# A spectral filter with a gated convolution on one core: low parts of y subtracted by GpSimd in the last 13 blocks, and the last two blocks' convolution taken one block at a time

## The chip, the core and the metric

The kernel runs on one core of a Trainium2 chip. The core has five engines that run side by side, each through its own list of instructions in a fixed order: TensorE (PE, matrix products), VectorE (DVE), ScalarE (ACT), GpSimd (POOL) and SyncE (SP, which here only starts transfers). They wait for each other through semaphores. SBUF is the on-chip memory of 128 partitions; TensorE writes its products to PSUM, a second on-chip memory, from which VectorE and ScalarE fetch them. The metric is device time in microseconds (us) from the first to the last instruction of one execution.

## The reference

```python
def _attn_ref(x, w_r, w_i, b_r, b_i):
    X = np.fft.rfft(x, axis=1)
    Yr = Xr @ w_r - Xi @ w_i + b_r
    Yi = Xr @ w_i + Xi @ w_r + b_i
    Yr = np.sign(Yr) * np.maximum(np.abs(Yr) - lam, 0.0)   # Yi alike, lam = 0.01
    y = np.fft.irfft(Y, n=x.shape[1], axis=1)

def _moe_ref(x, w_val, conv_w, w_out):          # x is the y above
    for k in range(K):                           # K = 5
        gate_pre += conv_w[k][None, None, :] * xp[:, k:k + S, :]
    gate = 1.0 / (1.0 + np.exp(-gate_pre))
    val = x @ w_val
    return (gate * val @ w_out).astype(np.float32)
```

x has 8 batches of 3200 positions and 256 channels, in float32. Each batch is transformed along its positions, mixed with complex 256 x 256 matrices, shrunk towards zero, and transformed back to y. Then a causal convolution of five taps per channel, through a sigmoid, gates the product of y with w_val; the gated values are multiplied by w_out.

## The kernel before

The Fourier transform is done by matrix products in two stages (64 x 50 positions), through two scratch tensors in DRAM (a_dram and z_dram). The result of the way back stands in SBUF as y_sb, channels on partitions. What follows is done in 8 blocks a batch, each of 400 positions in 2 halves of 128 channels, so 800 elements a partition. A block is written (b, k): batch b, block k, both from 0. The last two batches are 6 and 7.

For each pair of blocks, `conv` makes the gate's argument in a tile `acc`: ScalarE multiplies by the first tap (L1017), VectorE adds four taps for each channel half (L1020: one instruction of 800 elements, y_sb and acc in SBUF), and ScalarE takes the sigmoid (L1030). For each block, `gated` makes the values v_ps = y @ w_val on TensorE, VectorE multiplies them with the sigmoid (L1054, "the gate": v_ps in PSUM, acc in SBUF), and TensorE makes the output product o_ps with w_out, which ScalarE copies (L1079) and SyncE stores. The very last block's copy is shared by ScalarE and VectorE (L1073).

The products of matrices have two forms. In the split form a value is held as a high part, a rounded copy in a shorter format made by ScalarE (`split`, L505), and a low part, the difference, subtracted by VectorE (L507); twelve products of 400 columns (high x high, low weight x high, high weight x low, for two channel halves each way; L1003) make a block. In the whole-word form TensorE takes y or the gated product as it stands, with whole-word weights `w_late` that GpSimd sums once from their parts (L1090); four products, which appear as eight in the trace (L999), make a block and no split is needed. `LATE` lists the 16 blocks of the last two batches. The values of `LATE[6:]`, ten blocks, and the output products of `LATE[14:]`, two blocks, are in the whole-word form.

The order on each engine is found by the class `Plan` while the program is built: every piece of work has a due time `at`, an engine and a cost in ns, and a list schedule gives each engine's order. Due times come from the table `O`. The costs are the planner's own; what the chip takes stands in the trace. The split tile y_hl has two buffers, so the split of a block can run ahead of the product by two.

The first 752 us hold the forward and backward transforms of all batches, interleaved with the blocks of the batch before. After that only blocks (6, 3) and later are open.

Of the kernel before, what the change touches and what calls it, by code (L numbers as in the profile page):

```python
# [104 lines left out]
class Plan:  # L105
# [11 lines left out]
    def add(self, at, engine, busy, fn, uses=(), sets=(), new=None, delay=None, mode="r", kb=0, chain=None, extra=0, dmas=1, read=True, pair=None):  # L117
        n = len(self.pieces)
        before = set()
        for key in uses:  # L120
            before |= set(self.writers.get(key, ()))
        for key in sets:
            before |= set(self.readers.get(key, ())) | set(self.writers.get(key, ()))
        for key in uses:
            self.readers.setdefault(key, []).append(n)
        for key in sets:
            self.writers[key], self.readers[key] = [n], []
        p = dict(n=n, at=at, engine=engine, busy=busy, fn=fn, before=before, new=new or {}, mode=mode, kb=kb, extra=extra, dmas=dmas, read=read, pair=pair,
                 tiles={key[:2] for key in (*uses, *sets)}, delay=busy + LAND[engine] if delay is None else delay)
        p["behind"] = {self.last[chain]} if chain in self.last else set()  # L130
        if chain:
            self.last[chain] = n
        self.pieces.append(p)
        return n
# [159 lines left out]
def dve(n, copy=False):  # L294
    return 67 + n / (1.92 if copy else 0.96)


def act(n, kind="copy"):
# [23 lines left out]
     'val': 3.9688,  # L322
     'gate': -49.7775,
     'project': 6.045,
     'late_val': 6.023,
     'late_out': 14.484,
     'turn': -90.4451,
     'pre': -5.7976,
     'mix_sum': -1.2289,
# [11 lines left out]
     'u_val': 7,  # L341
     'u_conv': 8,
     'u_out': 9,
     'const': 1.7737,
     'load_x_0': 6.2588,
     'load_x_2': 11.2939,
     'load_x_3': 1.4455,
# [96 lines left out]
def fourier_filter_then_gated_conv(ctx: ExitStack, tc: tile.TileContext, x, w_r, w_i, b_r, b_i,  # L444
# [3 lines left out]
    sb = ctx.enter_context(tc.tile_pool(name="sb", bufs=2))  # L448
    ps = ctx.enter_context(tc.tile_pool(name="ps", bufs=1, space=bass.MemoryType.PSUM))
    dram = ctx.enter_context(tc.tile_pool(name="dram", bufs=2, space=bass.MemoryType.DRAM))  # L450
    LATE_VAL, LATE_OUT = set(LATE[int(O["late_val"]):]), set(LATE[int(O["late_out"]):])
    plan = Plan(SLOTS)
    add = plan.add
# [2 lines left out]
    def f32(ap):  # L456
        return ap.bitcast(F32)
# [37 lines left out]
    def two_banks(key, tag="ps_2"):  # L495
        return buffer(key, tag, [P, 2, 512])

    def split(at, n, key, src, high, low, uses=(), new=None, first=None):

        hl = key + ("high",), key + ("low",)  # L500

        def cast():
            if first:
                first()
            nc.scalar.copy(out=high(), in_=src())  # L505
        add(at, "ACT", act(n, "cast"), cast, uses, [hl[0]], new, chain=key[0])
        add(at + 0.001, "DVE", dve(n), lambda: nc.vector.tensor_tensor(out=low(), in0=src(), in1=f32(high()), op=ALU.subtract),  # L507
            [*uses, hl[0]], [hl[1]])
        return hl

# [173 lines left out]
    def of(name, b):  # L684
        return O[name] + O.get(f"{name}_{b}", 0.0)
# [254 lines left out]
    def y_at(k, c, tap=H0):  # L940
        return y_of(k, tap)[:, c]
# [64 lines left out]
    def conv(b, kk, at):  # L1006
        k = 2 * kk
        here = sorted({*y_keys(k, 1), *y_keys(k + 1, 1)})
        kg = ("acc", (b, kk))
        w = 2 * MB * N2  # L1010
        acc = lambda c: tl[kg][:, c]
        wide = lambda c, j: pair(y_sb, (MB * k + j) * N2, (N1 - 2 * MB - 2 * MB * k) * N2, w)[:, c]

        def first(c):
            if c == 0:
                tl[kg] = room(kg, "acc", 4 * TB).rearrange("p (c h n) -> p c h n", c=2, h=NH)
            nc.scalar.mul(acc(c), wide(c, 0), cw_sb[:, c, 0:1])  # L1017

        def tap(c, j):
            nc.vector.scalar_tensor_tensor(out=acc(c), in0=wide(c, j), scalar=cw_sb[:, c, j:j + 1], in1=acc(c), op0=ALU.mult, op1=ALU.add)  # L1020
        for c in range(2):
            add(at + of("conv", b) + 0.01 * c, "ACT", act(2 * TB, "conv"), lambda c=c: first(c), [*here, ("cw", 0, 0)],
                [kg + (c, e) for e in range(2)], {kg: "acc"} if c == 0 else None, chain="conv")
        for j in range(1, KC):
            for c in range(2):
                add(at + of("conv", b) + 0.02 * j, "DVE", 61 + dve(2 * TB), lambda c=c, j=j: tap(c, j), here,
                    [kg + (c, e) for e in range(2)],
                    delay=961 + (130 if j == KC - 1 else 0))
        for c in range(2):
            add(at + of("conv", b) + 0.15, "ACT", act(2 * TB, "sigmoid"), lambda c=c: nc.scalar.activation(  # L1030
                out=acc(c), in_=acc(c), func=AF.Sigmoid), (), [kg + (c, e) for e in range(2)])

    def gated(b, k, at):
        bk = (b, k)
        here = y_keys(k, 0)
        ky, kg, kv, kh, kp, ko = (("y_hl", bk), ("acc", (b, k // 2)), ("v_ps", bk), ("gated", bk), ("o_ps", bk), ("o", bk))
        if bk in LATE_VAL:
            vs = [*here, ("w_late", 0, 0)]
            vm = lambda e: matrix(kv, e, lambda: w_late[0], lambda h, c: y_at(k, c), True)
        else:  # L1040
            src = lambda: y_of(k)
            view = lambda j: tl[ky][:, j].rearrange("p c (h n) -> p c h n", h=NH)
            vs = [*split(at + of("y", b), 2 * TB, ky, src, lambda: view(0), lambda: view(1), here, {ky: "y_hl"},
                         lambda: buffer(ky, "y_hl", [P, 2, 2, TB], F32R)), ("w", "w_val", "high"), ("w", "w_val", "low")]
            vm = lambda e: matrix(kv, e, wv_sb, lambda h, c: tl[ky][:, h, c, :], False)
        for e in range(2):
            add(at + of("val", b), "PE", 1344 if bk in LATE_VAL else 1101, lambda e=e: vm(e), vs, [kv + (e,)],
                {kv: "ps_2"} if e == 0 else None, chain="val")


        ours = [kg + (c, k % 2) for c in range(2)]
        part = lambda: pair(tl[kg].rearrange("p c h n -> p c (h n)"), k % 2 * MB * N2, (3 - 2 * (k % 2)) * MB * N2, MB * N2)
        by_half = lambda ap: ap.rearrange("p c (h n) -> p c h n", h=NH)
        add(at + of("gate", b), "DVE", dve(2 * TB), lambda: nc.vector.tensor_tensor(  # L1054
            out=part(), in0=by_half(tl[kv][:, :, 0:TB]), in1=part(), op=ALU.mult), [kv + (0,), kv + (1,)], ours)
        if bk in LATE_OUT:
            gs = [*ours, ("w_late", 0, 0)]
            om = lambda e: matrix(kp, e, lambda: w_late[1], lambda h, c: part()[:, c], True)
        else:
            gs = [*split(at + of("gate", b) + 0.1, 2 * TB, kh, part, lambda: by_half(tl[kh][:, 0]), lambda: by_half(tl[kh][:, 1]),  # L1060
                         ours, {kh: "g_hl"}, lambda: buffer(kh, "g_hl", [P, 2, 2, TB], F32R)),
                  ("w", "w_out", "high"), ("w", "w_out", "low")]
            om = lambda e: matrix(kp, e, wo_sb, lambda h, c: tl[kh][:, h, c, :], False)
        for e in range(2):
            add(at + of("project", b), "PE", 1344 if bk in LATE_OUT else 1101, lambda e=e: om(e), gs, [kp + (e,)],
                {kp: "ps_2"} if e == 0 else None)
        cols = out[b].rearrange("(c p) n -> p c n", p=P)
        dst = [cols[:, :, lo:lo + MB * N2] for lo in (k * TB, (NB - 1 - k) * TB + MB * N2)]
        kind = at + of("project", b) + 0.1
        if bk == (B - 1, NB - 1):  # L1070
            def keep(e):
                o = buffer(ko, "o", [P, 2, TB]) if e == 0 else tl[ko]
                (nc.scalar.copy, nc.vector.tensor_copy)[e](out=o[:, e], in_=tl[kp][:, e, 0:TB])  # L1073
            for e, eng in enumerate(("ACT", "DVE")):
                add(kind, eng, act(TB) if e == 0 else dve(TB), lambda e=e: keep(e), [kp + (e,)], [ko + (e,)],
                    {ko: "o"} if e == 0 else None)
                add(kind, "SP", 700, lambda e=e: [nc.sync.dma_start(out=dst[h][:, e], in_=block(tl[ko][:, e])[:, h]) for h in range(NH)], [ko + (e,)], (), kb=200, dmas=2, read=False)
            return
        add(kind, "ACT", act(2 * TB), lambda: nc.scalar.copy(out=buffer(ko, "o", [P, 2, TB]), in_=tl[kp][:, :, 0:TB]),  # L1079
            [kp + (0,), kp + (1,)], [ko + (0,)], {ko: "o"})  # L1080
        add(kind, "SP", 900, lambda: [nc.sync.dma_start(out=dst[h], in_=blocks(tl[ko])[:, :, h]) for h in range(NH)], [ko + (0,)], (), kb=400, dmas=2, read=False)
# [117 lines left out]
```

## Time and profile before

| | |
|---|---|
| time, median of 3 runs | 847.21 us (846.08 to 847.69) |
| the profiled execution's own time | 845.59 us |
| its span on the core | 843.8 us |
| TensorE busy | 825.3 us (98%) |
| VectorE busy | 735.9 us (87%) |
| ScalarE busy | 596.3 us (71%) |
| GpSimd busy | 147.9 us (18%) |
| granted TensorE clock | 0.993 of full speed |

Times in the trace's views are in us from the span's start, and a row gives start, duration, engine, line, operation, and output <- inputs. A group's row gives a count (x48), the busy time, the mean of one in ns, and the idle time just before with what ended it. TensorE's rows overlap, since its products are pipelined; the chain of waits shows what each added. GpSimd's busy time before is nearly all the issue of transfers; after 642 us it has nothing more to do.

### The profile page before, as it was taken

Reading aid. Unit: us, or ns where it says so; the run is one execution under the profiler, and the core shown is the slowest. Engines: PE = TensorE matmul, PEld = TensorE weight load, DVE = VectorE, ACT = ScalarE, POOL = GpSimd, SP = SyncE. Lnnn points to the kernel's source line nnn. Section 1 sums busy time; section 2 is a strip of 40 time slices with the busy share of each in tenths; the row PEclk is TensorE's granted clock in tenths of the full one; section 3 lists DMA queues with packets and bytes.
Section 4 is the critical chain, followed back from the end, with each engine's and each line's share of the span. In section 5 each row is a group of like instructions: output and inputs, shape, how many; then the busy total and the mean of one; then the engine's idle time right before and its main releaser. Section 6 shows DMA issues by size and latency. Waiting matters only on the chain.

```text
span 843.8 us, 24474 instructions
## 1 busy us (share of the span) xinstructions
PE 825.3 (98%) x10036; PEld 715.3 (85%) x10036; DVE 735.9 (87%) x1006; ACT 596.3 (71%) x903; POOL 147.9 (18%) x284
## 2 busy tenths in 40 slices
PE   9999989999999999999999999999999999999997
PEld 5777768888889889898989988898888899999775
DVE  3367796989988999989988999889989899979994
ACT  2246566787877787778787777778775778777662
POOL 5332222201221121302211031301212000000000
PEclk9899999999999999999999999999999999999999
DMA  8898999867877786767966696758875455336313
GB/s 191 246 238 229 266 230 271 224 173 223 241 187 199 204 225 193 196 171 219 266 204 173 180 251 194 222 144 217 249 211 157 136 154 161 108 100 172 109 64 98
DMA packets 122665, 162.33 MB, mean 192 GB/s; under 512 B 16496, under 2 KB 102266, under 8 KB 122554
## 3 DMA queue, kind: packets, MB, share of 16 engines
q1 hardware_dynamic: 109706, 134.73, 57.1%
q0 software_dynamic: 12848, 26.04, 12.0%
q8 instruction: 80, 1.31, 0.7%
q14 instruction: 31, 0.25, 0.1%
HBM read 82.06 MB, written 78.64 MB: 190 GB/s over the span
## 4 chain that ended last, share of the span: by engine, by line
PE 75%; DVE 14%; DMA 6%; ACT 2%; issue 2%; POOL 1%; SPq 0%; DVEq 0%; ACTq 0%; POOLq 0%
PE y_ps L903 14%; PE o_ps L1003 13%; PE v_ps L1003 11%; PE y_p L969 9%; PE y_ps L907 7%; DVE acc L1020 4%; PE z_ps L858 4%; PE s L789 4%; PE p L716 4%; PE v_ps L999 3%; DMA x<-in_x 3%; DMA a_dram<-s 2%; DVE s L736 2%; PE p L480 1%; DVE xs L838 1%
## 5 line engine op out<-in xcount | busy, mean ns | idle before, releaser
L1020 DVE SCALAR_TENSOR_TENSOR acc<-y_sb,cw_sb,acc 128x800 f32<-128x800 f32 x256 | 262.4, 1044 | 31.7 <-ACT acc L1017 30.1
L903 PE MATMUL y_ps<-w_sb,xs 128*128 128x256 f32 x1152 | 153.0, 284 | 2.0 <-DVE y_ps L909 1.7
L903 PEld LDWEIGHTS y_ps<-w_sb,xs 128*128 128x128 f32 x1152 | 142.5, 189 | 12.3 <-issue 5.6
L1003 PE MATMUL o_ps<-gated,wo_sb 128*128 128x400 f32 x744 | 150.7, 350 | 0.2 <-DVE s L736 0.2
L1003 PEld LDWEIGHTS o_ps<-gated,wo_sb 128*128 128x128 f32 x744 | 133.5, 188 | 5.7 <-issue 2.3
L1003 PE MATMUL v_ps<-y_hl,wv_sb 128*128 128x400 f32 x648 | 130.0, 347 | 0.4 <-ACT y_sb L973 0.4
L671 POOL DMA_DIRECT2D x<-in_x x142 | 74.5, 530 | 295.2 <-PE p L723 286.1
L1003 PEld LDWEIGHTS v_ps<-y_hl,wv_sb 128*128 128x128 f32 x648 | 114.8, 188 | 4.0 <-ACT sx L830 0.8
L736 DVE TENSOR_TENSOR s<-p,s 128x512 f32<-128x512 f32 (+2 forms) x144 | 88.6, 624 | 28.9 <-ACT s L731 16.9
L671 POOL DMA_DIRECT2D a_dram<-s x122 | 63.9, 528 | 196.9 <-DVE s L736 166.6
L969 PE MATMUL y_p<-g_sb,zl 100*64 100x100 f32 x2048 | 96.5, 251 | 0.8 <-ACT acc L1030 0.8
L915 ACT ACTIVATE tp<-y_ps,nlam 128x512 f32<-128x512 f32 (+1 forms) x104 | 69.8, 671 | 38.5 <-PE y_ps L903 37.0
L969 PEld LDWEIGHTS y_p<-g_sb,zl 100*64 100x64 f32 x2048 | 88.9, 137 | 9.5 <-issue 4.7
L907 PEld LDWEIGHTS y_ps<-w_sb,xs 128*128 128x128 f32 x576 | 76.4, 189 | 21.3 <-issue 8.9
L907 PE MATMUL y_ps<-w_sb,xs 128*128 128x256 f32 x576 | 87.7, 289 | 5.2 <-ACT y_ps L885 2.8
L917 DVE SCALAR_TENSOR_TENSOR tp<-y_ps,tp 128x512 f32<-128x512 f32 (+1 forms) x104 | 68.4, 661 | 7.1 <-ACT tp L915 6.9
L505 ACT CAST gated<-acc 128x800 fp32r<-128x800 f32 x62 | 53.5, 863 | 27.4 <-DVE acc L1054 27.0
L729 ACT COPY s<-p 128x512 f32<-128x512 f32 x64 | 37.5, 595 | 42.4 <-PE p L723 31.6
L716 PE MATMUL p<-x,f_sb 50*64 50x512 f32 x256 | 65.5, 599 | 1.3 <-DMA x<-in_x 0.8
L723 PE MATMUL p<-x,f_sb 50*64 50x512 f32 x240 | 65.9, 601 | 0.0
L1054 DVE TENSOR_TENSOR acc<-v_ps,acc 128x800 f32<-128x800 f32 x64 | 62.8, 981 | 3.4 <-PE v_ps L999 1.7
L1079 ACT COPY o<-o_ps 128x800 f32<-128x800 f32 x63 | 51.9, 823 | 19.2 <-PE o_ps L1003 13.9
(95 smaller groups left out, 1172.0 us busy)
## 6 DMA issues: line engine op xcount, KB each, us to landing
out<-o SPq DMA_DIRECT2D x126, 200.0 KB
a<-a_dram SPq DMA_DIRECT2D x96, 256.0 KB
z_dram<-z_t SPq DMA_DIRECT2D x48, 512.0 KB
zl<-z_dram SPq DMA_DIRECT2D x64, 384.0 KB
x<-in_x SPq DMA_DIRECT2D x63, 192.0 KB
a_dram<-s POOLq DMA_DIRECT2D x61, 192.0 KB, 4.3
a_dram<-s SPq DMA_DIRECT2D x59, 192.0 KB
x<-in_x POOLq DMA_DIRECT2D x57, 192.0 KB, 5.2
```

Source lines behind the costliest of these rows:

```text
L671: eng.dma_start(out=out[lo:hi], in_=in_[lo:hi])
L716: nc.tensor.matmul(p[k * HP:(k + 1) * HP, 0, :], f1_sb[half(0), 0:HP], xt[half(0), k * 512:(k + 1) * 512], start=True, stop=True)
L723: nc.tensor.matmul(dst, f1_sb[half(1), 0:HP], back[:, 2 * k:2 * k + 2, :], start=True, stop=True)
L736: nc.vector.tensor_tensor(out=st()[lo:hi, h, n], in0=p[lo:hi, 0, n], in1=st()[lo:hi, 1, n], op=(ALU.add, ALU.subtract)[h])
L903: nc.tensor.matmul(p[:, 1 - r, :], xm(hx, c, r, i), w_sb[:, m, hw, c, :], start=False, stop=k == 5, skip_group_check=True)
L907: nc.tensor.matmul(tl[ky][:, 0], sm(hx, c, i), w_sb[:, 0, hw, c, :], start=False, stop=k == 5, skip_group_check=True)
L915: nc.scalar.activation(out=buffer(kt, "tp", [P, 2, D])[:, 0:n], in_=tl[ky][:, 0:n], func=AF.Relu, bias=nlam)
L917: add(at + 0.2, "DVE", dve(n * D), lambda: nc.vector.scalar_tensor_tensor(out=tl[kt][:, 0:n], in0=tl[ky][:, 0:n], scalar=LAM, in1=tl[kt][: ...
L969: nc.tensor.matmul(dst[e * HP:(e + 1) * HP], zt[0:Q, m, c * P + e * HP:c * P + (e + 1) * HP], g, start=True, stop=True)
L1003: nc.tensor.matmul(p[:, e, 0:TB], w[:, hw, c, e * P:(e + 1) * P], src(hy, c), start=n == 0, stop=n == 5)
L1020: nc.vector.scalar_tensor_tensor(out=acc(c), in0=wide(c, j), scalar=cw_sb[:, c, j:j + 1], in1=acc(c), op0=ALU.mult, op1=ALU.add)
L1054: add(at + of("gate", b), "DVE", dve(2 * TB), lambda: nc.vector.tensor_tensor(out=part(), in0=by_half(tl[kv][:, :, 0:TB]), in1=part(), op= ...
```

## The change

Four things are edited.

1. `late_pool` is 3: for the blocks of `LATE[3:]`, that is (6, 3) to (6, 7) and the whole of batch 7, thirteen in all, the low part of y is subtracted by GpSimd instead of VectorE. The planner costs that at 4.9 ns an element.
2. `late_val` is 16: no block's values are in the whole-word form any more. The ten blocks that were get a cast on ScalarE and a subtract on GpSimd.
3. `late_out` is 12: the output products of the last four blocks, not two, are in the whole-word form.
4. The last pair's convolution is made by `conv_last`, block by block: each tap is an instruction of 400 elements for one block instead of 800 for the pair, and the second block is due 2.0 later.

```diff
-     'late_val': 6.023,
-     'late_out': 14.484,
+     'late_val': 16,
+     'late_out': 12,
...
+     'conv_last': 2.0, 'late_pool': 3, 'const': 1.7737,
...
+    LATE_POOL = set(LATE[int(O["late_pool"]):])
...
-    def split(at, n, key, src, high, low, uses=(), new=None, first=None):
+    def split(at, n, key, src, high, low, uses=(), new=None, first=None, pool=False):
...
-        add(at + 0.001, "DVE", dve(n), lambda: nc.vector.tensor_tensor(out=low(), in0=src(), in1=f32(high()), op=ALU.subtract),
+        eng, busy = ("POOL", 4.9 * n) if pool else ("DVE", dve(n))
+        add(at + 0.001, eng, busy, lambda: (nc.gpsimd if pool else nc.vector).tensor_tensor(out=low(), in0=src(), in1=f32(high()), op=ALU.subtract),
             [*uses, hl[0]], [hl[1]])
...
+        if (b, k) == (B - 1, NB - 2):
+            for i in range(2):
+                conv_last(b, k + i, at, kg)
+            return
...
+    def conv_last(b, k, at, kg):
+        here = y_keys(k, 1)
+        at += O["conv_last"] * (k % 2)
...
+        for c in range(2):
+            add(at + of("conv", b) + 0.01 * c, "ACT", act(TB, "conv"), lambda c=c: nc.scalar.mul(acc(c), y_at(k, c, 0), cw_sb[:, c, 0:1]),
+                [*here, ("cw", 0, 0)], [kg + (c, k % 2)], {kg: "acc"} if c == 0 and k % 2 == 0 else None, chain="conv")
+            for j in range(1, KC):
+                add(at + of("conv", b) + 0.02 * j, "DVE", 61 + dve(TB), lambda c=c, j=j: nc.vector.scalar_tensor_tensor(
+                    out=acc(c), in0=y_at(k, c, j), scalar=cw_sb[:, c, j:j + 1], in1=acc(c), op0=ALU.mult, op1=ALU.add),
+                    here, [kg + (c, k % 2)], delay=61 + dve(TB) + (190 if j == KC - 1 else 60))
...
-                         lambda: buffer(ky, "y_hl", [P, 2, 2, TB], F32R)), ("w", "w_val", "high"), ("w", "w_val", "low")]
+                         lambda: buffer(ky, "y_hl", [P, 2, 2, TB], F32R), bk in LATE_POOL), ("w", "w_val", "high"), ("w", "w_val", "low")]
```

On every engine the order is the one of before up to the split of block (6, 3), at about 753 us; from there to the end it is laid anew. In the changed kernel the lines have moved: the taps are L1022 (L1051 in `conv_last`), the gate L1078, the subtracts L509, the split products L1005, the whole-word products L1001.

VectorE's list around blocks (6, 3) to (6, 5), before: `acc` with taps is the convolution, `acc<-v_ps` the gate, `gated` the subtract of the gated product and `y_hl` that of y.

```order
L1054 TENSOR_TENSOR acc<-v_ps,acc 128x2x400
L507 TENSOR_TENSOR y_hl<-y_sb,y_hl 128x800
L507 TENSOR_TENSOR gated<-acc,gated 128x800
L1020 SCALAR_TENSOR_TENSOR acc<-y_sb,cw_sb,acc 128x800
L1054 TENSOR_TENSOR acc<-v_ps,acc 128x2x2x200
L507 TENSOR_TENSOR y_hl<-y_sb,y_hl 128x800
L1020 SCALAR_TENSOR_TENSOR acc<-y_sb,cw_sb,acc 128x800
L507 TENSOR_TENSOR gated<-acc,gated 128x800
```

The same place of the change:

```order
L1078 TENSOR_TENSOR acc<-v_ps,acc 128x2x400
L509 TENSOR_TENSOR gated<-acc,gated 128x800
L1022 SCALAR_TENSOR_TENSOR acc<-y_sb,cw_sb,acc 128x800
L1078 TENSOR_TENSOR acc<-v_ps,acc 128x2x2x200
L1022 SCALAR_TENSOR_TENSOR acc<-y_sb,cw_sb,acc 128x800 x2
L509 TENSOR_TENSOR gated<-acc,gated 128x800
```

The subtracts of y are gone from VectorE's list. They stand on GpSimd's, behind the sum of the late weights; the waits at a row's end name the engines waited for.

```order
L1114 TENSOR_TENSOR w_late_8760<-wv_sb_72 128x512 [waits DMAHW1_49,DMAHW0_49,PE_49]
L1114 TENSOR_TENSOR w_late_8760<-wo_sb_73 128x512
L509 TENSOR_TENSOR y_hl_10165<-y_sb_78,y_hl_10165 128x800 [waits DVE_49,Activation_49]
L509 TENSOR_TENSOR y_hl_10233<-y_sb_78,y_hl_10233 128x800 [waits DVE_49,Activation_49]
L509 TENSOR_TENSOR y_hl_10283<-y_sb_78,y_hl_10283 128x800 [waits Activation_49]
```

There are 13 such rows to the program's end, each waiting for ScalarE's cast, and nothing else on GpSimd among them.

TensorE's list at the end, before (v_ps are the values, o_ps the output products):

```order
L1003 MATMUL o_ps<-gated,wo_sb 128x400 x12
L999 MATMUL v_ps<-y_sb,w_late 128x400 x6
L1003 MATMUL o_ps<-gated,wo_sb 128x400 x12
L999 MATMUL v_ps<-y_sb,w_late 128x400 x2
L999 MATMUL o_ps<-acc,w_late 128x400 x8
```

and of the change:

```order
L1005 MATMUL o_ps<-gated,wo_sb 128x400 x12
L1005 MATMUL v_ps<-y_hl,wv_sb 128x400 x12
L1001 MATMUL o_ps<-acc,w_late 128x400 x4
L1005 MATMUL v_ps<-y_hl,wv_sb 128x400 x12
L1001 MATMUL o_ps<-acc,w_late 128x400 x4
```

The values come from split parts up to the last block, and the output products of blocks (7, 4) and (7, 5) have become whole-word ones; those of the last two blocks follow them as before.

More of the change, by code (lines that the diff above doesn't have):

```diff
@@ L343 @@
      'u_out': 9,
-     'const': 1.7737,
+     'conv_last': 2.0, 'late_pool': 3, 'const': 1.7737,
      'load_x_0': 6.2588,
@@ L1031, in conv, with acc @@
                 out=acc(c), in_=acc(c), func=AF.Sigmoid), (), [kg + (c, e) for e in range(2)])
+    def conv_last(b, k, at, kg):
+        here = y_keys(k, 1)
+        at += O["conv_last"] * (k % 2)
+        def acc(c):
+            if kg not in tl:
+                tl[kg] = room(kg, "acc", 4 * TB).rearrange("p (c h n) -> p c h n", c=2, h=NH)
+            return pair(tl[kg].rearrange("p c h n -> p c (h n)"), k % 2 * MB * N2, (3 - 2 * (k % 2)) * MB * N2, MB * N2)[:, c]
+        for c in range(2):
[5 more added lines that the diff above has]
+                    here, [kg + (c, k % 2)], delay=61 + dve(TB) + (190 if j == KC - 1 else 60))
+            add(at + of("conv", b) + 0.15, "ACT", act(TB, "sigmoid"), lambda c=c: nc.scalar.activation(out=acc(c), in_=acc(c), func=AF.Sigmoid),
+                (), [kg + (c, k % 2)])
     def gated(b, k, at):
```

## The prediction

> **What bounds the kernel now.** I read the page first: its busy line, its slices, and the shares of the chain that ended last.
>
> ```profile
> span 843.8 us, 24474 instructions
> PE 825.3 (98%) x10036; PEld 715.3 (85%) x10036; DVE 735.9 (87%) x1006; ACT 596.3 (71%) x903; POOL 147.9 (18%) x284
> DVE  3367796989988999989988999889989899979994
> POOL 5332222201221121302211031301212000000000
> PE 75%; DVE 14%; DMA 6%; ACT 2%; issue 2%; POOL 1%; SPq 0%; DVEq 0%; ACTq 0%; POOLq 0%
> ```
>
> TensorE is the bound as a whole, and GpSimd is idle in the last nine slices. But all that the change edits lies after 752 us, so its price must be read there. The view of busy time by stretches gives, in columns, the length, then PE, PEld, DVE, ACT and POOL, each with its instructions:
>
> ```profile
> 760.00:780.00 20.00, 20.00 (x206) 19.23 (x205) 20.00 (x24) 13.88 (x19) 0.00 (x0) 1.00 0.59 168
> 780.00:800.00 20.00, 20.00 (x135) 15.51 (x134) 19.93 (x22) 14.26 (x18) 0.00 (x0) 1.00 0.34 103
> 800.00:820.00 20.00, 20.00 (x135) 15.51 (x134) 19.18 (x21) 11.93 (x16) 0.00 (x0) 1.00 0.26 83
> 752.80:834.75 81.95, 81.95 (x592) 67.86 (x592) 75.50 (x81) 52.02 (x68) 0.00 (x0) 1.00 0.38 116
> ```
>
> The reader is to see two full engines. The last line is the stretch that I use: from the end of the last spectral work to the end of the last gate product. TensorE has no gap in its 81.95 us, VectorE hardly more than 6.5. Taking time off TensorE alone gains only what VectorE can follow; time put on VectorE costs soon. The chain in order of time (start, us, what) shows TensorE's steps:
>
> ```profile
> 773.57 2.18 PE v_ps L1003 x12
> ...
> 816.42 2.69 PE v_ps L999 x8
> 819.11 2.17 PE o_ps L1003 x12
> ...
> 833.71 5.39 PE o_ps L999 x16
> 839.10 0.03 ACTq L1073
> ```
>
> A block's values cost 2.18 us from split parts and 2.69 from whole words, and an output product from split parts 2.17.
>
> **TensorE's part of the change.** Ten blocks leave the whole-word form: 10 x (2.69 - 2.18) = 5.1 us less. Two more output products enter it: 2 x (2.69 - 2.17) = 1.0 more. Net 4.1 us less, and worth that only while TensorE stays the bound.
>
> **VectorE's own work.** Its groups in that stretch, and some of its rows in order of time:
>
> ```profile
> L1020 DVE SCALAR_TENSOR_TENSOR acc<-y_sb,cw_sb,acc 128x800 f32<-128x800 f32 x48 | 48.5, 1043 | 3.0 <-ACT acc L1017 2.9
> L1054 DVE TENSOR_TENSOR acc<-v_ps,acc 128x800 f32<-128x800 f32 x15 | 14.8, 984 | 3.4 <-PE v_ps L999 1.7 <-ACT acc L1030 0.9 <-PE v_ps L1003 0.7
> L507 DVE TENSOR_TENSOR gated<-acc,gated 128x800 fp32r<-128x800 f32 x14 | 13.8, 982 | 0.0
> L507 DVE TENSOR_TENSOR y_hl<-y_sb,y_hl 128x800 fp32r<-128x800 f32 x3 | 2.9, 982 | 0.0
> ```
>
> ```profile
> 768.65 5.86 DVE L1020 SCALAR_TENSOR_TENSOR acc<-y_sb,cw_sb,acc 128x800 f32<-128x800 f32 x6
> 774.43 0.98 DVE L1054 TENSOR_TENSOR acc<-v_ps,acc 128x800 f32<-128x800 f32 x1
> 775.33 1.04 DVE L1020 SCALAR_TENSOR_TENSOR acc<-y_sb,cw_sb,acc 128x800 f32<-128x800 f32 x1
> ...
> 833.75 0.99 DVE L1054 TENSOR_TENSOR acc<-v_ps,acc 128x800 f32<-128x800 f32 x1 [1.21 <-PE v_ps L999]
> ```
>
> Successive rows overlap a little, so I cost by distance of starts: a tap (774.43 - 768.65) / 6 = 0.96, a gate or subtract 775.33 - 774.43 = 0.90. By these the stretch holds 48 x 0.96 for taps, 15 x 0.90 for gates, 13 subtracts of the gated product (the first of the 14 lies before it) and 3 of y (16 x 0.90), and 0.3 for a copy: 74.3 us, which leaves 7.6 free. The change removes the 3 subtracts of y and 2 of the gated product: 5 x 0.90 = 4.5. The last two blocks' taps become 16 of half length for 8 whole ones; a 400-element tap has no row, and I take half of 0.96 with at most 0.06 more each, 0 to 1 us in all. VectorE's own work falls to 70 us. ScalarE gains ten casts of y and loses two of the gated product, all under 0.9 us: 52.02 becomes some 60 of 82, still hidden.
>
> **GpSimd's part, the one that decides.** Thirteen subtracts of 800 elements, both inputs in SBUF, are new on GpSimd. The page has one pair of such instructions, the sum of the late weights (POOL rows), and beside it stands this on VectorE:
>
> ```profile
> 639.63 1.30 POOL L1090 TENSOR_TENSOR w_late<-wv_sb 128x512 f32<-128x512 f32 x1
> 640.90 1.30 POOL L1090 TENSOR_TENSOR w_late<-wo_sb 128x512 f32<-128x512 f32 x1
> ```
>
> ```profile
> 638.71 0.98 DVE L1054 TENSOR_TENSOR acc<-v_ps,acc 128x800 f32<-128x800 f32 x1
> 639.61 3.45 DVE L507 TENSOR_TENSOR y_hl<-y_sb,y_hl 128x800 fp32r<-128x800 f32 x1
> 642.98 0.68 DVE L842 TENSOR_TENSOR xs<-sx,xs 128x512 fp32r<-128x512 f32 x1
> L507 DVE TENSOR_TENSOR y_hl<-y_sb,y_hl 128x800 fp32r<-128x800 f32 x54 | 55.4, 1025 | 1.0 <-ACT y_hl L505 1.0
> ```
>
> The subtract of y that takes 0.98 us elsewhere took 3.45 here: 2.47 us longer, while GpSimd was busy from 639.63 to 642.20. It ended at 643.06, 0.86 after GpSimd's end, which is one whole subtract. It did no work while GpSimd ran. In the group of 54 this row explains the mean: (1025 - 982) x 54 = 2.3 us, so it is the one such case. Both instructions read two SBUF operands. The gate product (L1054) reads one of its two from PSUM; whether it too is blocked no row shows.
>
> So I price a subtract on GpSimd as a hold of 1.30 x 800 / 512 = 2.03 us, 13 x 2.03 = 26.4 us in all, in which VectorE's taps and gated subtracts (some 56 of its 70 us) stand still. Behind a blocked tap wait the later taps, then the sigmoid on ScalarE, the gate, the cast and the output product on TensorE; VectorE becomes the bound.
>
> What may lie beside a hold is a gate (0.90), or time in which VectorE waits anyway. Bounds:
> - Low: every hold covers a whole gate, 13 x 0.90 = 11.7, and no other gap stays. 70 + 26.4 - 11.7 = 84.7 us for the 81.95: 2.8 more.
> - High: no gate is covered, and all 7.6 us of gaps stay. 70 + 26.4 + 7.6 = 104.0: 22 more.
> - My value: six gates covered (5.4) and 3 us of gaps, as the first taps still wait for their y: 70 + 26.4 - 5.4 + 3 = 94.0: 12.1 more. I choose the middle because of two rows that pull apart. GpSimd began its second instruction while VectorE had long been waiting, so a holder that has its next instruction ready keeps what it holds; VectorE with its runs of taps would then keep GpSimd out until a gate comes, and most holds would begin at a gate. Against it, taps that wait for the one before leave openings amid the run.
>
> The end gains a little. Before, 4.36 us lie between the last gate's end (834.74) and TensorE's end (839.10), as it still has two blocks of output products to do (5.39 us). With VectorE behind, the first of them is done when the last gate ends, and one block of 2.69 remains, some 0.1 for the hand-over: 1.6 less.
>
> **Sum**: +12.1 - 1.6 = 10.5 us. TensorE's 4.1 us turn into idle time. The profiled execution took 845.59 us, so 856.1; it lies 1.62 below the median of 847.21, so I add that: **857.7 us**. Own bounds: 845.59 + 2.8 - 1.6 + 1.6 = 848.4, and 845.59 + 22 - 1.6 + 1.6 = 867.6.
>
> The Trainium skill has a rule here ("SBUF — State Buffer", section Who interferes with whom): a VectorE instruction with two SBUF inputs and a GpSimd instruction that reads SBUF exclude each other, for the whole instruction of whoever came first. The trace agrees with the exclusion (3.45 for 0.98), not plainly with the turn, since GpSimd's second instruction went ahead of a VectorE one that was waiting. With strict turns, a hold would start at the end of whichever instruction runs; gates being 13.5 of 70 us, only a fifth of the 11.7 would be covered, 2.3 us, and the sum would be 3.1 higher, 860.8.
>
> The skill's "GPSIMD Engine Reference" (section Performance versus the Vector engine) gives some 2.6 cycles per element at 1.2 GHz for two inputs. An estimate by that page is 1.73 us for 800 elements, and 13 x 0.30 = 3.9 us less than my sum; the row of 1.30 us for 512 elements decides for 2.03.
>
> **Rivals.**
> 1. *VectorE isn't held up.* The one long row could be a peculiarity of two instructions back to back, and a lone subtract could slip between the taps. Then TensorE stays the bound and keeps its 4.1 us, less some 0.4 for new waits on low parts: 845.59 - 3.7 + 1.6 = 843.5. For it: GpSimd is otherwise idle, and VectorE's own 70 us fit the 78 left. Against it: the row of 3.45. It decides where a subtract costs VectorE less than (81.95 + 1.6 - 73) / 13 = 0.81 us, and even with a gate over it a hold of 2.03 costs 1.13. Chance 0.08.
> 2. *It comes out even.* Holds fall on gates and on the gaps before the first taps, costing near 0.8 us each: 847, within 0.2% of before. For it: gates alternate with taps in the new order, one per block. Against it: it needs all 13 to fall so. Chance 0.06.
> 3. *The hold is longer than a proportion says.* The planner's new line costs the subtract at 4.9 ns an element, 3.92 us. If that is the hold, 13 x (3.92 - 2.03) = 24.6 us come on top: 882. Against it: that figure may include waiting, and the measured pair gives 2.54 ns. Chance 0.06.
>
> **How the numbers follow.** My forecast has 0.80. Some 0.2% (1.7 us) is what a measurement here can tell from no change. Faster is rival 1, 0.08; the same is rival 2, 0.06; slower is the forecast and rival 3, 0.86. The range from 848 to 867 is the forecast's bounds, leaving out the three rivals, 0.20.
>
> **What would show it.** Right: taps of about 3 us in the last 90 us, each beside a subtract on POOL; TensorE with 10 us or more of idle time there, its releasers VectorE or GpSimd; the last gate some 12 us later. The step on the hold is wrong if POOL's subtract takes clearly other than 2 us when VectorE is free; that on cover is wrong if gates beside a hold are long too. The whole is wrong if taps stay at 1.04 us while POOL works beside them.

## The result

The change made the kernel slower: 858.52 us median (856.03 to 860.71) against 847.45 (846.08 to 849.15), a ratio of 1.0141 with a 95% interval of 1.0117 to 1.0164. The forecast was 857.7. The profiled execution took 856.03 us with a span of 854.2, 10.4 more than the span of before. The page of the changed kernel, the rows that answer to those shown of before:

```profile
span 854.2 us, 24580 instructions
PE 826.6 (97%) x10068; PEld 726.2 (85%) x10068; DVE 748.8 (88%) x1009; ACT 603.1 (71%) x915; POOL 175.6 (21%) x297
PE 75%; DVE 16%; DMA 3%; ACT 2%; issue 2%; SPq 0%; POOL 0%; DVEq 0%; ACTq 0%
```

The totals hardly tell anything. The stretches do (length, then PE, PEld, DVE, ACT and POOL; the column after the last bracket is the granted TensorE clock):

```profile
760.00:780.00 20.00, 17.88 (x178) 17.13 (x178) 19.96 (x18) 12.53 (x18) 6.40 (x4) 0.91 0.43 128
780.00:800.00 20.00, 17.12 (x144) 16.50 (x141) 19.89 (x18) 12.86 (x18) 5.23 (x3) 0.86 0.35 104
800.00:820.00 20.00, 19.30 (x150) 18.55 (x148) 19.80 (x18) 15.47 (x20) 6.59 (x4) 0.97 0.22 69
```

VectorE is as full as before, with 18 instructions in a stretch where it had 21 to 24. TensorE, full before, now has 2 to 3 us of idle time in two of the three.

VectorE's groups after 752.8 us show which of its instructions grew:

```profile
L1022 DVE SCALAR_TENSOR_TENSOR acc<-y_sb,cw_sb,acc 128x800 f32<-128x800 f32 x40 | 50.6, 1294 | 2.2 <-ACT acc L1019 1.9
L509 DVE TENSOR_TENSOR gated<-acc,gated 128x800 fp32r<-128x800 f32 x11 | 14.9, 1357 | 0.9 <-ACT gated L506 0.9
L1078 DVE TENSOR_TENSOR acc<-v_ps,acc 128x800 f32<-128x800 f32 x15 | 14.7, 983 | 2.5 <-ACT acc L1054 1.2 <-PE v_ps L1005 0.7 <-ACT acc L1036 0.6
```

Taps went from 1043 to 1294 ns and gated subtracts from 982 to 1357. Gates, which read one operand from PSUM, stayed at 983. Laid beside GpSimd's rows, the longer instructions can be told one by one:

```profile
759.24 1.91 POOL L509 TENSOR_TENSOR y_hl<-y_sb,y_hl 128x800 fp32r<-128x800 f32 x1 [4.37 <-ACT y_hl L506]
763.45 2.19 POOL L509 TENSOR_TENSOR y_hl<-y_sb,y_hl 128x800 fp32r<-128x800 f32 x1 [2.29 <-ACT y_hl L506]
774.53 1.93 POOL L509 TENSOR_TENSOR y_hl<-y_sb,y_hl 128x800 fp32r<-128x800 f32 x1 [8.90 <-ACT y_hl L506]
...
803.77 1.90 POOL L509 TENSOR_TENSOR y_hl<-y_sb,y_hl 128x800 fp32r<-128x800 f32 x1 [10.14 <-ACT y_hl L506]
...
817.09 2.65 POOL L509 TENSOR_TENSOR y_hl<-y_sb,y_hl 128x800 fp32r<-128x800 f32 x1 [6.93 <-ACT y_hl L506]
```

```profile
752.02 0.99 DVE L1078 TENSOR_TENSOR acc<-v_ps,acc 128x800 f32<-128x800 f32 x1 [0.71 <-PE v_ps L1005]
...
759.47 3.51 DVE L1022 SCALAR_TENSOR_TENSOR acc<-y_sb,cw_sb,acc 128x800 f32<-128x800 f32 x2
762.89 0.98 DVE L509 TENSOR_TENSOR gated<-acc,gated 128x800 fp32r<-128x800 f32 x1
763.80 2.69 DVE L1022 SCALAR_TENSOR_TENSOR acc<-y_sb,cw_sb,acc 128x800 f32<-128x800 f32 x1
...
774.37 0.98 DVE L1078 TENSOR_TENSOR acc<-v_ps,acc 128x800 f32<-128x800 f32 x1
775.27 3.00 DVE L1022 SCALAR_TENSOR_TENSOR acc<-y_sb,cw_sb,acc 128x800 f32<-128x800 f32 x2
...
844.56 0.99 DVE L1078 TENSOR_TENSOR acc<-v_ps,acc 128x800 f32<-128x800 f32 x1 [1.21 <-ACT acc L1054]
```

Two taps alone take 2.00 us. Beside the subtract of 759.24 they took 3.51, and the tap of 763.80 took 2.69 for 1.04. The subtract of 774.53 began with a gate: the gate took its usual 0.98, and the taps behind it only 1.00 more. Going through all 13 in this way, VectorE's instructions are 15.9 us longer in sum, 1.22 for each subtract of 1.90.

### The profile page after: what moved, and what is told of

It reads as the page before. It is cut to its first block, busy times and chain, and to the rows that moved or that the text cites. A ratio compares the mean times of both kernels' runs of the same rounds, so it can differ in the third digit from the quotient of the medians.

```text
span 854.2 us, 24580 instructions
## 1 busy us (share of the span) xinstructions
PE 826.6 (97%) x10068; PEld 726.2 (85%) x10068; DVE 748.8 (88%) x1009; ACT 603.1 (71%) x915; POOL 175.6 (21%) x297
## 4 chain that ended last, share of the span: by engine, by line
PE 75%; DVE 16%; DMA 3%; ACT 2%; issue 2%; SPq 0%; POOL 0%; DVEq 0%; ACTq 0%
PE y_ps L905 14%; PE v_ps L1005 12%; PE o_ps L1005 12%; PE y_p L971 8%; DVE acc L1022 8%; PE y_ps L909 7%; PE p L718 5%; PE s L791 5%; PE z_ps L860 5%; PE p L481 2%; DVE gated L509 2%; DVE s L738 2%; DMA a_dram<-s 2%; DVE acc L1078 2%; DMA a<-a_dram 1%
## 5 line engine op out<-in xcount | busy, mean ns | idle before, releaser
L1022 DVE SCALAR_TENSOR_TENSOR acc<-y_sb,cw_sb,acc 128x800 f32<-128x800 f32 x248 | 264.6, 1085 | 30.9 <-ACT acc L1019 29.1
L1005 PE MATMUL o_ps<-gated,wo_sb 128*128 128x400 f32 x720 | 149.0, 356 | 9.3 <-DVE acc L1078 5.0
L1005 PE MATMUL v_ps<-y_hl,wv_sb 128*128 128x400 f32 x768 | 155.6, 350 | 0.5 <-ACT y_sb L975 0.4
L1005 PEld LDWEIGHTS o_ps<-gated,wo_sb 128*128 128x128 f32 x720 | 133.5, 194 | 13.3 <-DVE acc L1078 5.4
L1005 PEld LDWEIGHTS v_ps<-y_hl,wv_sb 128*128 128x128 f32 x768 | 138.7, 190 | 4.6 <-ACT sx L832 0.8
L506 ACT CAST y_hl<-y_sb 128x800 fp32r<-128x800 f32 x64 | 55.0, 860 | 26.3 <-PE v_ps L1005 25.8
```

Source lines behind the costliest of these rows:

```text
L1005: nc.tensor.matmul(p[:, e, 0:TB], w[:, hw, c, e * P:(e + 1) * P], src(hy, c), start=n == 0, stop=n == 5)
```

## The experiments

The theory was that a GpSimd instruction with SBUF operands keeps VectorE's instructions with two SBUF operands out while it lasts. Its rivals: that TensorE waits for low parts which a slower engine brings late, or loses by a lower clock; and that the other edits or the new order cost the time.

### GpSimd writes, but reads next to nothing

```diff
-        add(at + 0.001, eng, busy, lambda: (nc.gpsimd if pool else nc.vector).tensor_tensor(out=low(), in0=src(), in1=f32(high()), op=ALU.subtract),
-            [*uses, hl[0]], [hl[1]])
...
+            if pool:
+                nc.gpsimd.tensor_copy(out=low()[:, 0, 0, 0:1], in_=f32(high())[:, 0, 0, 0:1])
+                for _ in range(2):
+                    nc.gpsimd.memset(f32(low()), 0.0)
...
```

> The changed kernel, but GpSimd only writes: instead of subtracting, it copies one element of the high part (so that it still waits for ScalarE's cast) and fills the low part with zeros twice, about as long as the subtract of 1.90 us; the low parts are left out of the values. Order and waits of every other engine are the same. Theory (GpSimd's two SBUF operands keep VectorE's two-operand instructions out): nothing keeps VectorE out, taps are back at 1.04 us, TensorE is the bound again and keeps the split form's gain; 843 to 845 us, some 14 below the change. Rival (TensorE waits because low parts come late from the slower engine, or because its clock falls): the low parts come as late as in the change, so 855 to 860 us.

The low parts of y in the last 13 blocks are zeros here, so this kernel leaves out a part of the result. It took 842.40 us against 847.77, a ratio of 0.994 (0.992 to 0.996): 16 us below the change, and faster than before. The median is 0.6 below the expected range; the 4.1 us of TensorE lie within the interval. GpSimd was about as long at work for each block as in the change, and VectorE's rows are back to their length (VectorE's and GpSimd's groups after 752.8 us and 745 us):

```profile
L1029 DVE SCALAR_TENSOR_TENSOR acc<-y_sb,cw_sb,acc 128x800 f32<-128x800 f32 x41 | 41.7, 1048 | 3.0 <-ACT acc L1026 2.7
L516 DVE TENSOR_TENSOR gated<-acc,gated 128x800 fp32r<-128x800 f32 x12 | 11.8, 987 | 0.9 <-ACT gated L506 0.9
```

```profile
L514 POOL MEMSET y_hl<- 128x800 f32 x26 | 20.0, 768 | 1.5
L512 POOL CAST y_hl<-y_hl 128x1 fp32r<-128x1 f32 x13 | 3.7, 281 | 157.2 <-ACT y_hl L506 157.2
```

The order, the waits, ScalarE's casts and the time at which low parts arrive are as in the change; what was taken away are the operands read. VectorE's work is too: from the first gate behind the common part to the end of the last gate both kernels have the same 83 instructions in the same order. The busy time of the two stretches (columns as above), the change first:

```profile
752.02:845.55 93.53, 84.61 (x621) 79.05 (x620) 88.19 (x83) 58.52 (x78) 27.43 (x13) 0.91 0.33 99
754.86:832.47 77.61, 77.54 (x620) 72.36 (x619) 72.09 (x83) 58.32 (x78) 23.61 (x39) 1.00 0.41 121
```

They are 93.5 and 77.6 us long, and the 15.9 between them are what the 13 instructions of the change are longer in sum. So reading is what costs, and late low parts are not.

### The subtracts back on VectorE

This kernel is edited from the changed one.

```diff
-     'conv_last': 2.0, 'late_pool': 3, 'const': 1.7737,
+     'conv_last': 2.0, 'late_pool': 16, 'const': 1.7737,
```

> The changed kernel with the 13 subtracts of y on VectorE; values from split parts, late output products and the convolution by blocks as in the change. Theory: VectorE's own 70 us rise by 13 x 0.90 to 81.7, and with 4 to 7 us of gaps it is the bound at 86 to 89 for the 82 of before: 850 to 854 us, below the change, since 0.90 on VectorE is less than the about 1.15 us that a hold cost it. Rival (late low parts): they come sooner, so TensorE's gain shows: 843 to 845 us. Rival (the split form's other work, casts and order): no better than the change, 857 to 860 us.

854.83 us, a ratio of 1.0085 (1.0058 to 1.0112) to before, 7.1 us more; 0.8 above the range. VectorE does its 13 subtracts itself in this group of the same stretch,

```profile
L509 DVE TENSOR_TENSOR y_hl<-y_sb,y_hl 128x800 fp32r<-128x800 f32 x13 | 12.8, 986 | 0.2 <-ACT y_hl L506 0.2
```

and the kernel is still faster than with GpSimd's help: 1.0085 (at most 1.0112) against the change's 1.0141 (at least 1.0117). Ten blocks more of 0.90 on VectorE, less two gated subtracts, are 7.2 us, and 7.1 is what came out: the gaps took in nothing of it, against what I had expected.

### Spare subtracts in the kernel of before

The second of these two kernels has `range(2)` in the edit's last loop.

```diff
+            def spare(j):
+                if j == 0:
+                    buffer(ky, "y_hl", [P, 2, 2, TB], F32R)
+                out = tl[ky][:, j].rearrange("p c (h n) -> p c h n", h=NH)
+                nc.gpsimd.tensor_tensor(out=out, in0=y_of(k), in1=y_of(k), op=ALU.subtract)
+            for j in range(1):
+                add(at + of("y", b) + 0.001, "POOL", 4.9 * 2 * TB, lambda j=j: spare(j), here, [ky + (j,)], ...)
```

> The kernel of before plus one subtract of 800 elements on GpSimd for each of the ten blocks whose values are in the whole-word form, y minus y, into a tile that nothing reads. Nobody waits for it but the next writer of y. Theory: each hold costs VectorE about what one cost in the change (1.15 us of 1.90), 11.5 us, of which VectorE's gaps of before take 3 to 5: 853 to 857 us, or more where fewer holds fall on gates. Rival (only waiting for the low part costs): as before, 846 to 849 us.

> The same with two spare subtracts for each of the ten blocks, 20 in all. Theory: the second ten find no gaps left, 12 to 19 us more than with one each: 866 to 876 us. Rival (only waiting costs, or the effect saturates): under 858 us.

One spare each: 858.24 us, 1.0136 (1.0087 to 1.0186), 10.5 us more. Two each: 869.69, 1.0263 (1.0220 to 1.0306), 21.9 more. Work whose result nobody uses, on an engine that was idle, costs as much as the whole change. The first value is 1.2 above its range, the second inside its own. No engine waits for GpSimd's subtracts in the first one's trace, and ScalarE once, for 1.1 us, in the second's. VectorE's groups after 752.8 us, of the kernel with one and then of that with two:

```profile
L1020 DVE SCALAR_TENSOR_TENSOR acc<-y_sb,cw_sb,acc 128x800 f32<-128x800 f32 x49 | 57.9, 1213 | 2.9 <-ACT acc L1017 2.7
L507 DVE TENSOR_TENSOR gated<-acc,gated 128x800 fp32r<-128x800 f32 x14 | 15.1, 1078 | 0.0
L987 DVE COPY y_sb<-y_sb 128x392 f32<-128x392 f32 x1 | 1.7, 1676 | 0.0
```

```profile
L1020 DVE SCALAR_TENSOR_TENSOR acc<-y_sb,cw_sb,acc 128x800 f32<-128x800 f32 x49 | 65.7, 1371 | 2.9 <-ACT acc L1017 2.7
L507 DVE TENSOR_TENSOR gated<-acc,gated 128x800 fp32r<-128x800 f32 x14 | 18.9, 1354 | 0.0
```

With one, the taps are (1213 - 1043) x 49 = 8.3 us longer, the gated subtracts (1078 - 982) x 14 = 1.3, the copy 1.3: 10.9. With two, 16.1 and (1354 - 982) x 14 = 5.2 and 0.4 on three subtracts of y: 21.7. The time grew by 10.5 and 21.9. What VectorE loses, the kernel loses; its gaps, waits for ScalarE's first taps and for TensorE's values, don't shrink in return.

### A spare copy, with one operand

```diff
-                nc.gpsimd.tensor_tensor(out=out, in0=y_of(k), in1=y_of(k), op=ALU.subtract)
+                nc.gpsimd.tensor_copy(out=out, in_=y_of(k))
```

> The kernel of before with one spare copy of y on GpSimd for each of the ten whole-word blocks: the same places and the same 800 elements out as the spare subtract, but one SBUF operand in. Theory (any read of SBUF by GpSimd keeps VectorE's two-operand instructions out, for as long as it lasts): VectorE's taps beside a copy are longer by up to the copy's own time, which at one operand I take as half of the subtract's, 0.8 to 1.0 us; with gates and gaps as cover 2 to 5 us in all, 849 to 853 us. Rival (only a second operand on GpSimd contends): as before, 846 to 849 us, taps at 1.04 us.

851.38 us against 846.75, 1.0048 (1.0032 to 1.0065). Two of GpSimd's rows and VectorE's taps after 752.8 us:

```profile
794.75 0.86 POOL L1045 CAST y_hl<-y_sb 128x800 fp32r<-128x800 f32 x1 [11.91 <-ACT y_sb L973]
796.84 1.29 POOL L1045 CAST y_hl<-y_sb 128x800 fp32r<-128x800 f32 x1 [1.23 <-ACT y_sb L973]
```

```profile
L1020 DVE SCALAR_TENSOR_TENSOR acc<-y_sb,cw_sb,acc 128x800 f32<-128x800 f32 x49 | 53.0, 1113 | 2.9 <-ACT acc L1017 2.7
```

One operand is enough, and the cost grows with the time for which GpSimd reads: copies of 0.86 us, 4.6 us for ten; spare subtracts of 1.62, 10.5 for ten.

### The other edits

The late output products and the convolution by blocks alone, edited from the changed kernel:

```diff
-     'late_val': 16,
+     'late_val': 6.023,
...
-     'conv_last': 2.0, 'late_pool': 3, 'const': 1.7737,
+     'conv_last': 2.0, 'late_pool': 16, 'const': 1.7737,
```

> The kernel of before with two of the four edits alone: the output products of the last four blocks, not two, in the whole-word form, and the last pair's convolution block by block. Values and subtracts are as before, and GpSimd gets nothing. Theory (the loss is the hold alone): TensorE 2 x 0.52 = 1.0 us more in the stretch that it bounds, at the end up to 1 us less since the last gate can come sooner; 846 to 849 us, no difference from before. Rival (these edits or their order cost a part of the loss): 850 us or more.

846.65 us against 846.75, 1.0002 (0.999 to 1.0015): no difference. And the change with the convolution by pairs:

```diff
-        if (b, k) == (B - 1, NB - 2):
+        if False:
```

> The changed kernel with the last pair's convolution as before, for the pair in instructions of 800 elements. Theory: VectorE has the same elements to go through, so within 1.5 us of the change: 857 to 860 us. Rival (the block by block form was a gain that hides a part of the loss, or a loss of its own): more than 2 us from the change on either side.

858.82 us, 1.0139 (1.0119 to 1.0159), where the change had 1.0141. Neither edit carries a part of the loss that these runs, to some 1 us for the first and 3 us for the second, could show.

### TensorE's clock

The trace of the change shows something that I hadn't counted with. After each of three gaps TensorE's products are slow; its rows around two, and the stretches of the first product behind the first gap, of a usual one, and of the first and the second behind the last:

```profile
767.44 3.87 PE L1005 MATMUL o_ps<-gated,wo_sb 128*128 128x400 f32 x12 [2.12 <-DVE acc L1078]
771.15 2.35 PE L1005 MATMUL v_ps<-y_hl,wv_sb 128*128 128x400 f32 x12
...
823.21 3.70 PE L1005 MATMUL o_ps<-gated,wo_sb 128*128 128x400 f32 x10 [3.92 <-DVE gated L509]
826.71 3.22 PE L1005 MATMUL v_ps<-y_hl,wv_sb 128*128 128x400 f32 x12
```

```profile
767.44:771.15 3.71, 3.71 (x13) 3.68 (x13) 3.71 (x5) 2.62 (x4) 0.00 (x0) 0.58 0.22 78
773.33:775.50 2.17, 2.17 (x13) 2.17 (x13) 2.13 (x4) 1.99 (x3) 0.97 (x1) 1.00 0.50 160
823.21:826.71 3.50, 3.50 (x10) 3.48 (x11) 3.50 (x4) 0.86 (x1) 0.00 (x0) 0.50 0.00 0
826.71:829.77 3.06, 3.06 (x13) 3.05 (x13) 2.73 (x5) 2.11 (x3) 0.00 (x0) 0.69 0.36 115
```

The granted clock is 0.50 to 0.58 through the first product behind a gap, some 0.7 through the second behind two of them, and 1.00 in the usual stretch. To see whether that costs time, I filled the gaps:

```diff
+    WARMED = {("o_ps", (6, 2)): 9, ("o_ps", (6, 6)): 12}
...
+        if e == 0 and key in WARMED:
+            zeros(p, WARMED[key], True)
...
+                if e == 0 and n == 2 and key == ("o_ps", (7, 2)):
+                    zeros(p, 17, False)
```

> The changed kernel with products of zeros in TensorE's three gaps: 9 before the output product of block (6, 2), 12 before that of (6, 6), 17 behind the second product of (7, 2). They are written over or add nothing. Theory (VectorE is the bound and TensorE's slow products after a gap, 3.87 us for 2.33 at a granted clock of 0.58, lie beside its work): the clock stays near 1.00 there, the output products take 2.3 to 2.6 us, and the time falls by at most 2 us, to 856 to 859. Rival (the fall of the clock is a large part of the loss): 1.5, 2.0 and 2.0 us and what follows come back, 5 us or more: 853 or below.

862.02 us, 1.0168 (1.0141 to 1.0195): by the median 3.5 us above the change, though the two intervals overlap, and not up to 2 below it. Its rows of TensorE say why:

```profile
769.84 3.84 PE L481 MATMUL o_ps<-zero_sb 128*128 128x128 f32 x18 [2.12 <-DVE acc L1083]
773.33 2.58 PE L1008 MATMUL o_ps<-gated,wo_sb 128*128 128x400 f32 x12
...
825.33 3.96 PE L481 MATMUL o_ps<-zero_sb 128*128 128x128 f32 x34
829.47 2.10 PE L1008 MATMUL o_ps<-gated,wo_sb 128*128 128x400 f32 x10 [0.18 <-DVE gated L509]
831.40 2.33 PE L1008 MATMUL v_ps<-y_hl,wv_sb 128*128 128x400 f32 x12
```

In the first two places the zeros had to wait for the same gate as the product (2.12 again), since only the gate frees the PSUM buffer into which they go; they ran behind the gap, not in it, and put the products off by 3.5 and 4.3 us; VectorE then waited 1.48 and 1.47 us for a sigmoid (its gates at 778.34 and 809.21), which it had not done there in the change. There the experiment failed. In the third place they did fill the gap, and the products behind it ran at full speed: 2.10 for ten instead of 3.70, then 2.33 instead of 3.22. No gain shows. The time from the gate that follows to the end of the last gate can be read from these rows of VectorE, the change first and then the filled kernel:

```profile
824.04 0.98 DVE L1078 TENSOR_TENSOR acc<-v_ps,acc 128x800 f32<-128x800 f32 x1
```

```profile
830.30 0.98 DVE L1083 TENSOR_TENSOR acc<-v_ps,acc 128x800 f32<-128x800 f32 x1
...
834.99 3.64 DVE L1056 SCALAR_TENSOR_TENSOR acc<-y_sb,cw_sb,acc 128x400 f32<-128x400 f32 x3
...
851.29 0.99 DVE L1083 TENSOR_TENSOR acc<-v_ps,acc 128x800 f32<-128x800 f32 x1 [1.21 <-ACT acc L1059]
```

From 824.04 to 845.55 it is 21.5 us in the change, from 830.30 to 852.28 it is 22.0 with TensorE kept fast. But the two stretches differ in more than the clock: VectorE's waits are 0.9 us shorter in the filled kernel (those of 0.29 and 0.62 at 829.10 and 831.69 of the change are gone), and one subtract of GpSimd fell on half-length taps (3.64 us for three that alone take 1.72) where in the change it fell on a wait and a gate. Without these 1.9 us the filled stretch would be 20.1 long; by this estimate the slow clock cost up to 1.4 us in this place, and the run doesn't show that it cost nothing.

For the two other gaps the trace of the change itself answers. VectorE has no wait from 758.56 to 828.81 us (it is busy for 69.86 of the 70.21 us from 758.60 to 828.81), so TensorE's slow products at 767.44 and 795.43 kept VectorE from nothing: there the fall of the clock lay beside VectorE's work.

### A try at a faster kernel

With GpSimd's help gone, only a balance of TensorE and VectorE is left. Two more blocks in the split form, on VectorE, with the convolution by blocks; this too is edited from the changed kernel:

```diff
-     'late_val': 16,
-     'late_out': 12,
+     'late_val': 8,
+     'late_out': 14,
...
-     'conv_last': 2.0, 'late_pool': 3, 'const': 1.7737,
+     'conv_last': 2.0, 'late_pool': 16, 'const': 1.7737,
```

> The kernel of before with the convolution by blocks, and with the values of two more blocks, (6, 6) and (6, 7), from split parts, their low parts subtracted by VectorE; the other eight late blocks in the whole-word form, nothing on GpSimd. Theory (TensorE is the bound until VectorE has no gaps left): TensorE 2 x 0.51 = 1.0 us less, VectorE 2 x 0.90 = 1.8 more, which its 7.6 us of gaps take: 845.7 to 846.9 us for 846.8 of before. Rival (VectorE's gaps sit where they can't be used): 846.8 to 849.

847.18 us against 846.77, 0.9998 (0.9977 to 1.0019): no difference. The median lies 0.3 above the theory's range and inside the rival's, and the interval is too wide to tell the two apart. No kernel here that does all of its work beat the kernel of before.

## Why the prediction was right, step by step

**Two full engines.** Right. Work put on VectorE cost at once, even with TensorE's 4.1 us taken off (the subtracts back on VectorE: 7.1 us more), and VectorE's time taken away by spare work came out one for one (10.9 and 21.7 us against 10.5 and 21.9).

**The hold.** The step that decided: right in kind, 7% too long. A subtract that found VectorE out of the way took 1.90 us, not 2.03, so the 13 held 24.7 us, not 26.4. Rival 3, 3.92 us, is out: the longest row is 2.65, and that includes a wait. Rivals 1 and 2 needed a price under 0.81 us a subtract, or near it; it was 1.22.

**What is covered.** I took six gates, 5.4 us. The rows give 24.7 - 15.9 = 8.8. Gates are not held up (983 ns), which I had left open; that makes 13 x 0.90 the most they could cover. Two holds, of 752.97 and 830.97, lay in part beside waits of VectorE for ScalarE, so not all of the 8.8 is gates.

**Who gets in first.** I thought that VectorE's runs of taps could keep GpSimd out. They don't: the subtract asked for at 763.45 waited 0.3 us for the gated subtract then at work, went in ahead of the next tap, and that tap took 2.69. The longest wait in 13 rows is some 0.75 us, less than one instruction. That is the turn that the Trainium skill gives ("SBUF — State Buffer", section Who interferes with whom). The 860.8 that I worked out by it took the holds to begin at random; they began at gates and gaps more often than that. The Trainium skill's "GPSIMD Engine Reference" (section Performance versus the Vector engine) gave an estimate of 1.73 us for the subtract; the trace has 1.90.

Nor does a holder with its next instruction ready keep what it holds, as I had read out of the pair before. Where the kernel with two spare subtracts each has four back to back, they and VectorE's instructions take turns:

```profile
783.50 8.58 POOL L1045 TENSOR_TENSOR y_hl<-y_sb 128x800 fp32r<-128x800 f32 x4 [1.29 <-ACT y_sb L973]
783.95 2.30 DVE L507 TENSOR_TENSOR gated<-acc,gated 128x800 fp32r<-128x800 f32 x1
786.17 4.53 DVE L1020 SCALAR_TENSOR_TENSOR acc<-y_sb,cw_sb,acc 128x800 f32<-128x800 f32 x2
```

No tap of that kernel took more than 2.31 us. The turns aren't strict: in the kernel with one spare each, the subtract of 798.25 took 3.20 us and let two VectorE instructions go ahead. Why both of GpSimd's went ahead in the pair before (3.45 us for 0.98) stays open.

**The gaps.** Wrong: I let them shrink from 7.6 to 3 us. The stretch must be measured from the first gate after the common part, since that gate came at 753.55 before and at 752.02 after, with the same order up to there. To the end of the last gate it is 81.2 us before and 93.5 after, 12.3 more, where I had 12.1. The busy time of this stretch before (that of the change stands with the first experiment):

```profile
753.55:834.74 81.19, 81.19 (x588) 67.11 (x587) 75.45 (x80) 51.71 (x66) 0.00 (x0) 1.00 0.38 114
```

VectorE was idle for 5.7 us before and for 5.3 in the change, so the gaps stayed. Of the 93.5, 15.9 are the holds' share, 5.3 gaps and the other 72.3 VectorE's own work, where I had 21.0, 3 and 70. My 70 was too small because distances of starts leave out small pauses (74.3 for a stretch before that the view shows busy for 75.50), and because a half-length tap takes 0.55 us. So the term of the holds was 5.1 too large, those of the gaps and of VectorE's own work 2.3 too small each: they cancelled.

**The end.** I took 1.6 us off. From the last gate's end (845.55) to TensorE's end it is 3.9 us now and was 4.36, so 0.5 came off. In the new order the output product of block (7, 6) stands behind the values of (7, 7), and so it began only at 843.91:

```profile
841.41 2.66 PE L1005 MATMUL v_ps<-y_hl,wv_sb 128*128 128x400 f32 x12
843.91 5.54 PE L1001 MATMUL o_ps<-acc,w_late 128*128 128x400 f32 x16
```

**The sum.** 12.3 - 0.5, less the 1.5 by which the common part ended sooner in this execution, are 10.3 for the 10.4 of the spans; by the medians it is 11.1. I had 10.5. The size is right partly by luck, as terms that missed by 2 to 5 us did so in opposite directions.

**TensorE's 4.1 us** became idle time, as forecast: 8.9 us of waits ahead of output products, a little under the 10 that I had named as a sign. That they are worth having when VectorE is left alone, rival 1's half, the kernel that only writes shows.

## What to carry to other kernels

Before work goes to an idle GpSimd, ask what VectorE does meanwhile. Where VectorE is busy with instructions that read two SBUF operands, the offloaded work returns to it as a hold, and here it returned as more: a subtract of 0.90 us on VectorE became 1.90 on GpSimd and 1.22 of VectorE's time. The trace had shown it before: one instruction of 3.45 us for 0.98, the only one such in its group of 54, beside the only two GpSimd instructions of the kind; an odd maximum in a group is worth a look at what stands beside it.

## What the runs showed of the hardware that I had not expected

- A VectorE copy with one SBUF operand is held too: 1676 ns for 349 to 360 (L987, 392 elements of float32) where it stood beside a spare subtract. The Trainium skill ("SBUF — State Buffer", section Who interferes with whom) says that of copies in a mode that uses two ports; whether this copy ran in one, no run here shows.
- GpSimd held VectorE by reading, not by writing: two fills of 800 elements, 1.54 us, left the taps at 1048 ns.
- After a gap of 2.1 to 3.9 us, TensorE's granted clock was 0.50 to 0.58 through the next product, some 3.5 to 4.2 us, and some 0.7 through the one behind it where the gap was 2.9 or 3.9 us. A gap of 0.97 us in the kernel of before (643.71) left it at 1.00. Where products of zeros filled the gap (829.47 of the filled kernel) it stayed at 1.00.
- A subtract of y from itself took GpSimd 1.62 us and of two different tiles 1.90, both of 800 elements.
